# A new table of order, engines and buffers for a two-layer attention kernel

## The chip, the cores and the metric

The kernel runs on one core of one Trainium2 chip, in one launch. The metric is device time in microseconds (us), from the start of the program to its end. All inputs come from HBM and the result is written back to HBM.

## The reference, cut to what matters

Two kinds of layer alternate, A, B, A, B, each added to the residual `x` of 2048 tokens by 512 channels, all in bf16. Both have 32 heads of 16 channels.

```python
x = A_x
x = x + A(layernorm(x), wq, wk, wv, wo, beta)
x = x + B(layernorm(x), wqkv, w_phi, wo)
x = x + A(layernorm(x), ...)      # the same weights again
x = x + B(layernorm(x), ...)

def A(x, ...):                    # four segments of 512 tokens
    for s in range(4):
        p = softmax(q_s @ k_s.T / 4 + causal mask)
        a_dot = p @ v_s
        a_mem = phi(q_s) @ M / (phi(q_s) @ z + 1e-6)   # phi(t) = t+1 if t>0 else exp(t)
        out_s = g * a_mem + (1 - g) * a_dot            # g = sigmoid(beta), per head
        M, z = M + phi(k_s).T @ v_s, z + sum(phi(k_s))
    return concat(out) @ wo

def B(x, ...):                    # not causal: needs all tokens' keys first
    phi_q = [softmax(q @ w_phi), softmax(-q @ w_phi)]  # over 16 channels
    phi_k = the same of k
    kv, z = phi_k.T @ v, sum(phi_k)
    return (phi_q @ kv / (phi_q @ z + 1e-6)) @ wo
```

## The kernel before, in words

Tokens are cut into 16 tiles of 128, and four tiles make a segment. The residual X stays in SBUF for the whole program. `build` records every step as an operation of a graph (`Graph.op`), about 2,750 of them, with the tiles that it reads and writes. A helper records each kind, so that one source line stands for many operations: `mm` (L341) and `pair` (L356) record matmuls on TensorE (PE), `act` (L366) an activation on ScalarE (ACT), `evac` a copy from PSUM to SBUF that may stand on ACT (L374) or on VectorE (DVE, L375), `tr` (L383) a transpose by DMA issued from SyncE (SP), `dma` (L387) a store.

The work runs in this order. For each segment of layer A: layer norm (`ln`, DVE statistics L590 and L591, the root on GpSimd, POOL, L598 and L600, the scaling on DVE L607 or L611), a transpose of the normed tile, the projections to k, q and v (`a_proj`), then attention (`a_att`): scores by PE into a PSUM tile, the exponential on ACT from PSUM to SBUF (tiles p, pF and pE), the product with the values on PE, the division on DVE (L405, L878), the addition of the memory part (`oadd`, L882, on DVE or POOL), a transpose of the result by DMA, the output projection on PE and the addition to X (`res`, L926, on DVE). The keys of layer B (`b_keys`) follow in the same segment: PE, an exponential (`kexp`) on ACT, sums and products on DVE (L985, L405, L1007), and KV sums. Only after all four segments can the queries of layer B run (`b_query`): two exponentials of each pair of groups on ACT, the denominators (`zm`, `zs`, `zp`, L1060, L1061, L1065, with logarithms and exponentials on ACT between them), the numerator on PE, a multiplication on DVE (`nmul`, L1087 or L1090), the sum of its two halves (`nadd`, L1093, on DVE or POOL), a transpose by DMA, the output projection and the addition to X. In the last layer each finished pair of tiles is stored to HBM from SP's queue.

What sets the order is a table, `ORDER` (L1177): compressed numbers that hold, for all operations at once, their order, the engine of each, and the buffer that each tile gets in its pool. `Graph.place` unpacks it and `Graph.emit` writes each engine's instructions in that order; an instruction waits on semaphores for the operations that it depends on, and for those that last used its buffer. Each engine, SP's queue included, works its list strictly in order, so an instruction that waits holds up all behind it. PSUM is four buffers of 128 x 1024 f32 (pool pD, named D in the profile), through which every matmul's result goes. `keep` (L678) records six pairs of matmuls on constants whose result is not used.

Of the kernel before, what the change touches and what calls it, by code (L numbers as in the profile page):

```python
# [1181 lines left out]
N~t4_$F6bi<z53o~J690wr~2?ia0jg7GhT3ikjpgZ=!6_5pMV;y`>D<KHC!xjjIrq~CwK{I?GKfp)u1x&%Im>s@`V4Mt}!wj5>{V)UzV-f6&q4*7a1{+`sJcjkq8=K=d
_$_9|7MKkIXW?vYjrkFg(ZXgZfL*975w^h|)CyZ-Ps)xtup8yXT-YB6;8xfMyP!LT!H4(}#)E>m8>YfE_!y@{F&u(<aTDah@9=xfjfHR(48<8x9K&!Fj>ddg6iZ-9EQR
xMKCXsgI2;8^TmxU=TG$8sVI7plC$Ix{!XO-s({MUIg>k4b4W*@L@El&i1pJW};CNh!V{k0q!B=#j9#9$l5k}xhEQ{r^JkG(nI1xwCNLq@Ma1ZQ-s+gIwPz9`ri!m!@q
ea+>I#V<Z#A;X_zr-IP9*v^W6rWzg99n{taW1`vyZ9r%f>|`1fYVV8tcjJdGKS-K@CujVa!g1WDHA22*Eo#s;ZHc6(o+V?OZn(NKEQ{Vp9;_r8cH3gBR$0`SPOSxZpuS
DaThM2g|r7B;|eT7EAbKj1aF`q<)R!^n6lFgdP#*SCl#e))Q48#YFvYB@n_hCeW^0_qbjrx*W(7<h_R?Y6{qS{g9g!N+=9JmFm1)s)SF^c9EwY?X&aWLGE|BNQd!yv<!
AuSqxlpIw_{bRMo+xN$HrO|2W!$e+Cb%LJk_R+v>W&0KHQIWs3KLO3N(hsQeCP?Q|McWi|^nwoIn%l2Ra1r;xRmd&+!G;rxFx_lPD4!(9ei8nWoYKNKA`pF%dnapXg_L
Ls7VdmeMquPQ=WDC6DGY%p^!tC@rJqG=om!4%$hN=rM&+1cg&HZlSI81HQonn1~8-VLpiKXeF(tHFOBq(+WC_M{zA}qa(PTBsHYtcpCe1Ken`+8qq0iOq*ykoxxocNoV
mqp2H$sl>74l-a~uoC0@i;bOFcn1l~vc=?SG|L%q2Vr{Xl6nsae(zKX@TIA23Y*D(j@<euD%73bl+JeFIL=F(h(OR=JHJeUh`K_0^Sc_0sB%Z7uvB<JHYyq$M&T0TGrs
VoOk6KYLuXebZk={$qeaR#2uQ#d_0rDhZxMsZvi&O3P*kL1NXla}xyn#hy5Iklj+)Q%3*5jsgrc^Qx3dR(8QC>9)sV4BL)_!4gBEqs(N;}twb(KM55ac!Q%b+|5{fRiw  # L1190
bxAHc2Jew<VWd;i75K6=gc@Zb(xjc`T^9l~(B%G9!b7s!MEvY@7rwW{nv+`*=LshsUXXmP1j?41}>drm5AvfX%oRKe5EUv-T_%iL~ecYI9a&>-(E>RP1%4cae@8M?LoZ
~<;j?Me|0EhBgUdM4bE{AbANANkC&ntNqALb+!k5}^=PD;t>5Jz$p$LAEZfDdv?Dj?paV|1JfiWZ!Ts)!R*RYdbf{*hmCOTI!^sTFtRPTZNha1n8Yl_)B-Xw7Z7Ew|$h
Y=jk+L}jsw*Yi=XA!>?u_&Nz8#k+irU-M6Vg9?el;x2XN_MDo2<~N+2Qt*59KHa2Sbd8?zF-XYA`8nUA<4{Z_;18*|IKkCKCPq<RkZ>YMfG8nK3Kl2%6kp&{qO|ycI&e
1*7G*?;2o+)C8kZFZp`NHOF7hQl&1d*JzvPOdg7}nP@DCg=KB7-3Lfqh6TuamzpV1doN7NOcQ$rCgVu^C%D|!dc@;N@w<;A-YTf`9wMI!MrH4?Y!OKKrniUy*wXd;@5%
Y22CimMzcqC_&0PkcxDML*GBd{6hNjc6;rro<wN_=b9k-XgxZ$?-&TkwPR8-%?7EO2ieNL~4;nq!sBz2hmw{6z}m7I10@~bJ0q)7Pt8hzt3GnSMdRV$e(aK(O!JSpYmP
)j6dguFiZ>==|vxrL1YwP@W-4<^c6itW|2i?72U-EkwfGZ-9!&DNDLH%#W(yV=MuTa5b-U4%|k^V@jcg(BSbclU3|wQ#V9daj1gl+U0F}w5#z*oF+qIA_xL{F6%)lQF-
g>ydBtooSxga2#8fd&Oc!&+T=AZGUp(e{V!l`^W{72Cjd;Q<#7wbVtQG6UI&nih;00o#SR@vUo8lqg61T-lu}VDU)#4Fv6dS}QaYSquTf|neO>7rO#V%0*c8UgShj>T4
D|U-LVy`$Q8miOcm^d!Zhz4?>I3W&-lj5vsr1pygqOm$88p_M!oVX$mi>u<ixF9Zx>!OitEH8>%^0vGt?#K_sN8&^AvG_!MDn1i;Wi$D?_(HrVo607#xojc76km&$vXy
KtzY*Vxuf%uazIY%Wis#~e`MtO&+Q_!Doop{(h?nA#cr0Ft*Wv@206vtx<rC3I_LqI-Phx<4Dn62*$dBcx@-sP5elDMhpG6(@MtmVz{vf)@A4QNHBs)kUrBt%6s;5Ar>
?*s-`l_kY(#VdolO)+p1<MfGL`BJH`K1h%VKRYCD4VMms-?2h$$oOMj3r~sIPxnwL=KhVGD3bW6UoFfu8b#>$fPn-ek<e4Z)7r=T((lr<qP>zwpMM_kMfm#AXCV!a<+U  # L1200
ZQ_55_wM-*B%kDD0OeZtQoHCotE`N||Wezz<&Xx0IE}2_?Cws{6<vp24wpEYhV>v}8&<VBHM&Fk`WiL5azLxW))j!F0s+@E>kxs13%Q(7%tSA@AQZlX{Cflpwa)i99uB
p<ptSlo>t1jw^JfjxM%JQr_r=H5Ga+;hj&#Mb+oE$H^Dyfy8A!o{G@@F|n#nbWiNLf&hlB4AWIZ?im#pHE$Lk(7WC8!`BtcR#cvbZcMOUMptmOLZ#$wIQD>ZER}TdIIO
D=W!!vbXA^`l|DCjJ&9BtGnuwN}?~T_tX`YR7dDY9j3$eWO+w*R_kScnNerb@2d~g2DwRgQyJw(c|sahQkT;GREQ4MndC`%TAq@HWo*4jZk8!@N}W|_(~IR2IaDo`R;`
rDG%8Z8lI!I%Oogjxol3{jpQ+DPcAY~XmY=9k)hc;J9+mINVJeMYAy>=7x`@s!hpQ1Pt^Q7ZuTtxe)EXJ3)9H`ZH>#*iufJ8@RS#8E7t=jeY_&{gk@wVn)n66Yy;K}EK
@CtP^cU)}%B-{Kuhm-lNDWkR)eQZWdY~Svcxs~hQaw>KbzYrMSCLia$NCffR8^DJWp15E$5-p*CAm!sHAm0Ymt{_!OK+E3WCAry&(@RFRykQks7Mv1qSY0-L++G&<@@>
rT}V51RgP3as-PaFg4Jj>PLJ37WC2}7){y!21yA-D<%jB-N~k92nzELhsGqAz`h}XTcgbTimYS#El?$~}^R-rGbvZp<Pto(#0zFl~R3WOgE~BUE^16aPuP^Az`Uka0FV
_3zr}{Jfx&A`WR}0j1wObyLKdLIaq8_8J>l?a~4ppyIRsBYRMoqeus-{2GAL-JnjQU!Cqc7_#I*}@?j>{S9s?MNq>RY<De64;`*YqK|M<!NDRdsz)U(z#GIrUhVS0nWk
okXQp#*EU|R8R-yHCa)yKCQ3I8#28bt<UHcI+dEGW~-+<naZFts!S@25_+Y6rqAlJYMiQ}e^%#oW;I2PS2yKUbyvTqr>QUXSGuOIr5ox-y0)&Y8f#&sxub9Em-+|&y<V
# [65 lines left out]
```

## Time and profile before

| | before |
|---|---|
| time, three runs | 462.59 us median, 462.41 to 462.62 |
| span of the profiled execution, first to last instruction | 461.2 us |
| PE busy | 437.7 us, 95% |
| ACT busy | 420.3 us, 91% |
| DVE busy | 416.2 us, 90% |
| POOL busy | 80.1 us, 17% |
| granted TensorE clock | 0.998 on average |

Times in the profile count from the start of the span. A row of the timeline gives start, length, engine, source line, operation, written and read tiles (buffer numbers left out), and in square brackets how long the engine stood idle before it and what ended that. A row of the table by stretch gives the busy time of each engine inside the stretch; "(x...)" is a count of instructions. SPq is SP's queue, where only the issue of a DMA takes time; PEld is the loading of weights.

### The profile page before, as it was taken

What the parts mean: (1) busy time and instruction counts of PE and PEld (TensorE: products, weight loads), DVE (VectorE), ACT (ScalarE), POOL (GpSimd) and SP (SyncE); (2) the same over time, 40 slices, a digit from 0 to 9 for tenths busy, and PEclk for the clock granted to TensorE, in tenths of its full rate; (3) what the DMA queues carried; (4) which work ended last, traced back from release to release, by engine and by line L of the source; (5) the groups of instructions that cost most, each with busy time, mean ns of one, the idle gap of its engine ahead of it and who ended that gap; (6) DMA issues with size and microseconds to landing.
All of it is one profiled execution on the core that took longest, in us unless ns stands there. A gap on an engine that the chain in (4) does not pass through costs nothing.

```text
span 461.2 us, 25354 instructions
## 1 busy us (share of the span) xinstructions
PE 437.7 (95%) x11716; PEld 295.6 (64%) x11716; DVE 416.2 (90%) x807; ACT 420.3 (91%) x542; POOL 80.1 (17%) x160
## 2 busy tenths in 40 slices
PE   8989899899999999998899999999999999998896
PEld 4456667667776776675456677677677677666553
DVE  6989998898889999898999899998899889998896
ACT  4999999899999998789699999999999999878991
POOL 2402021101221211102532031130221023110020
PEclk9999999999999999999999999999999999999999
DMA  8554642552233322100243443264113321200357
GB/s 247 127 150 80 127 63 37 75 96 54 50 46 54 46 40 36 37 3 4 48 54 78 71 85 72 49 96 61 26 39 49 50 39 27 48 14 1 50 121 180
DMA packets 90058, 30.37 MB, mean 66 GB/s; under 512 B 76640, under 2 KB 89952, under 8 KB 89952
## 3 DMA queue, kind: packets, MB, share of 16 engines
q1 hardware_dynamic: 89520, 28.48, 33.3%
q8 instruction: 92, 1.51, 1.4%
q10 hardware_dynamic: 432, 0.27, 0.2%
q14 instruction: 14, 0.11, 0.1%
HBM read 6.32 MB, written 2.10 MB: 18 GB/s over the span
## 4 chain that ended last, share of the span: by engine, by line
PE 48%; ACT 40%; DVE 6%; DMA 3%; issue 2%; SPq 0%
PE D L356 31%; ACT p L366 21%; PE D L341 15%; ACT pF L366 13%; ACT pE L366 5%; DMA p<-p 2%; PE D L662 2%; DVE X L926 1%; DMA X<-in_A_x_dram 1%; DVE p L1090 1%; DVE p L375 1%; DVE stats L590 1%; ACT pS L366 1%; DVE p L611 0%; DVE pK L375 0%
## 5 line engine op out<-in xcount | busy, mean ns | idle before, releaser
L366 ACT ACTIVATE p<-D 128x1024 bf16<-128x1024 f32 (+2 forms) x224 | 216.0, 1004 | 13.5 <-PE D L356 9.7
L366 ACT ACTIVATE pF<-D 128x896 bf16<-128x896 f32 x128 | 116.7, 940 | 2.8 <-PE D L341 2.5
L341 PE MATMUL D<-pK,pQ 64*128 64x256 bf16 (+3 forms) x1536 | 112.9, 243 | 4.1 <-ACT pF L366 1.0
L341 PEld LDWEIGHTS D<-pK,pQ 64*128 64x128 bf16 x1536 | 55.2, 94 | 40.7 <-ACT pF L366 5.4
L341 PE MATMUL D<-pV,pF 64*128 64x34 bf16 x1024 | 73.8, 175 | 0.4 <-ACT p L366 0.4
L341 PE MATMUL D<-pW,pF 64*128 64x34 bf16 x1024 | 71.3, 175 | 0.0
L341 PEld LDWEIGHTS D<-pV,pF 64*128 64x128 bf16 x1024 | 55.3, 93 | 2.3 <-ACT p L366 0.7
L341 PE MATMUL D<-pV,p 64*128 64x34 bf16 x1024 | 53.3, 176 | 0.3 <-issue 0.2
L366 ACT ACTIVATE pE<-D 128x768 bf16<-128x768 f32 x64 | 52.3, 831 | 1.4 <-PE D L341 1.0
L341 PEld LDWEIGHTS D<-pW,pF 64*128 64x128 bf16 x1024 | 51.9, 93 | 0.9
L341 PE MATMUL D<-pW,p 64*128 64x34 bf16 x1024 | 52.1, 176 | 0.0
L598 POOL TENSOR_SCALAR rstd<-mv 128x1 f32<-128x1 f32 x60 | 16.1, 272 | 205.9 <-DVE mv L591 205.5
L341 PEld LDWEIGHTS D<-pV,p 64*128 64x128 bf16 x1024 | 47.0, 93 | 3.3 <-issue 0.9
L341 PE MATMUL D<-tri,two 64*128 64x128 bf16 (+1 forms) x384 | 46.7, 234 | 0.4 <-issue 0.4
L341 PEld LDWEIGHTS D<-pW,p 64*128 64x128 bf16 x1024 | 45.2, 93 | 1.3
L590 DVE BATCH_NORM_STATS2 stats<-X 128x6 f32<-128x512 bf16 x64 | 42.9, 680 | 3.0 <-DMA X<-in_A_x_dram 2.5
L341 PE MATMUL D<-pV,pE 64*128 64x34 bf16 x512 | 44.9, 175 | 0.4 <-issue 0.4
L926 DVE TENSOR_TENSOR X<-X,D 128x1024 bf16<-128x1024 bf16 (+1 forms) x36 | 39.4, 1095 | 5.7 <-PE D L356 5.0
L341 PE MATMUL D<-pW,pE 64*128 64x34 bf16 x512 | 42.5, 175 | 0.1
L985 DVE TENSOR_REDUCE pS<-p 128x64 f32<-128x1024 bf16 (+1 forms) x36 | 38.8, 1088 | 1.8 <-ACT p L366 1.8
L375 DVE CAST p<-D 128x512 bf16<-128x512 f32 x48 | 31.1, 683 | 6.3 <-PE D L356 6.1
L356 PE MATMUL D<-WB_o,p 64*128 64x512 bf16 (+1 forms) x288 | 33.0, 353 | 2.7 <-issue 1.3
(115 smaller groups left out, 988.9 us busy)
## 6 DMA issues: line engine op xcount, KB each, us to landing
pW<-pV SPq DMA_DIRECT2D x16, 136.0 KB, 3.1
out_dram<-X SPq DMA_DIRECT2D x7, 256.0 KB, 2.8
X<-in_A_x_dram SPq DMA_DIRECT2D x3, 512.0 KB, 6.1
pX<-in_B_wqkv_dram SPq DMA_DIRECT2D x3, 512.0 KB, 4.6
p<-p SPq DMA_TRANSPOSE x76, 2.8
pX<-p SPq DMA_TRANSPOSE x54, 3.2
WA_k<-in_A_wk_dram SPq DMA_DIRECT2D x2, 256.0 KB, 6.3
WA_q<-in_A_wq_dram SPq DMA_DIRECT2D x2, 256.0 KB, 7.0
```

The source lines that it names most:

```text
L341: ins = e.matmul(out_ap, lhsT, rhs, start=st, stop=sp, tile_position=(basep(lhsT), basep(out_ap)))
L356: ins = e.matmul(out_ap, lhsT[64 * hf:64 * hf + 64], rhs[64 * hf:64 * hf + 64], start=k == 0 and i == 0, stop=k == 1 and i == len(lists[hf ...
L366: return self.g.op({"act": (dur, lambda e: e.activation(out_ap(), in_ap(), func, scale=scale))}, reads, writes, opens, label=label)
L375: "dve": ((340 if fast else n / 0.96 + 65), lambda e: e.tensor_copy(out_ap(), in_ap()))}
L590: v(lambda e: e.bn_stats(self.stats[:, t, :], self.X[:, t, :]), 602, [R("X", t)], [R("st", t)], label="bn")
L598: v(lambda e: e.tensor_scalar(rs, self.mv[:, t, 1:2], LN_EPS, None, op0=ALU.add), 170, [R("mv", t)], [R("rstd", t)], eng="pool", label="rstd")
L662: ins = e.matmul(D.t[c0:, r0 * 8:r0 * 8 + n], r[:, c0:], ones(r, n), start=True, stop=True, tile_position=(r0, c0))
L926: self.v(lambda e: e.tensor_tensor(X(), X(), src(), ALU.add), 65 + 512 * n / 0.96, pr + xr, xr, label="res")
L985: fn = lambda e, sgn=sgn, eo=eo, Z=Z, n=n: e.tensor_reduce(Z.t[:, 0:64 * n].rearrange("p (k s h) -> p k s h", k=n, s=2)[:, :, sgn, :], eo( ...
L1090: v(lambda e, N=N, Tm=Tm, w=w, shape=shape: e.tensor_tensor(shape(Tm.t[:]), shape(N.t[:]), w(), ALU.mult), 1131, [N, AB[(0, 0)], AB[(0, 1) ...
```

## The change

The operations, their arithmetic and the shape of every tile stay as they are. The string `ORDER` is replaced: another order, other engines for some operations, other buffers. One line out and one line in:

```diff
 ORDER = """
-c-rlG1GFYtlWpMm8fDwIZQHhO+qP}n=q}rAn`L%ab=S-MZdXt9|9jTVd+W_wli$7hWu9{~V#kghk(u{qfQFD5k^n<eNCu6dF*JchkQ&lJIzUJPDIpbPg!E7oN<u9FC<w
+c-qx?1-Ko>mhO`B;}UmwcXxMpcXxMpcXxL;NFeSC5r{wn2~Gm>0GaN6lKTP|?(k;j&ih{NbGoZ)S1<Y3zgAc66u^)X0D?e3dPoTwAQd!()Q|?!L0V`8jiCu7h9r;_2%17cs0oFj88iok
...
 """
```

The stages follow each other as before; within them operations stand some places earlier or later. Of the operations that may stand on either of two engines these move: four evacuations from ACT to DVE (near 95, 174, 249 and 405 us of the old profile) and one from DVE to ACT (near 390 us), so ACT has 49 instead of 52; four `oadd` from DVE to POOL and two back, six `nadd` from DVE to POOL (four of them near 235 to 253 us, two near 433 to 437 us); three settings of constants from POOL to DVE in the first 20 us.

ACT in layer A of the first pass, near 86 to 97 us of the old profile (p, pF and pE from D are exponentials of scores or keys, p from pK the one of `phi`, pK from D by L374 an evacuated q). Before:

```order
L366 ACTIVATE pE<-D 128x4x192
L366 ACTIVATE p<-D 128x1024 x2
L366 ACTIVATE p<-pK 128x1024
L366 ACTIVATE pF<-D 128x2x448 x2
L366 ACTIVATE p<-D 128x1024
L366 ACTIVATE pE<-D 128x4x192 x2
L374 ACTIVATE pK<-D 128x512
L366 ACTIVATE pF<-D 128x2x448 x2
L366 ACTIVATE p<-D 128x1024 x2
```

The same place in the new order:

```order
L366 ACTIVATE pE<-D 128x4x192
L366 ACTIVATE p<-D 128x1024
L366 ACTIVATE pF<-D 128x2x448
L366 ACTIVATE p<-D 128x1024
L366 ACTIVATE p<-pK 128x1024
L366 ACTIVATE pF<-D 128x2x448
L366 ACTIVATE p<-D 128x1024
L366 ACTIVATE pE<-D 128x4x192 x2
L366 ACTIVATE p<-D 128x1024
L366 ACTIVATE pF<-D 128x2x448
L366 ACTIVATE p<-D 128x1024
```

The first of the two pF moved ahead of an exponential of keys and of the one of `phi`, and the evacuation of q (L374) left ACT. On PE, the scores of both pF now stand ahead of the last half of a projection of k (WA_k); before, the second stood behind it.

DVE in the last stage, near 432 to 436 us (L1087 is `nmul`, L1093 `nadd`, L375 an evacuation, L1060, L1061 and L1065 the steps of the denominators). Before:

```order
L1093 TENSOR_TENSOR p<-p 128x512
L1087 TENSOR_TENSOR p<-p,pS 128x1024
L1065 TENSOR_TENSOR pS<-p,pS 128x8x16 x2
L1093 TENSOR_TENSOR p<-p 128x512
L1087 TENSOR_TENSOR p<-p,pS 128x1024
L375 CAST p<-D 128x512
L1093 TENSOR_TENSOR p<-p 128x512
L1060 TENSOR_TENSOR p<-p,D 128x256
```

The new order there:

```order
L1093 TENSOR_TENSOR p<-p 128x512
L1087 TENSOR_TENSOR p<-p,pS 128x1024 x2
L1065 TENSOR_TENSOR pS<-p,pS 128x8x16 x2
L375 CAST p<-D 128x512
L1060 TENSOR_TENSOR p<-p,D 128x256
L1087 TENSOR_TENSOR p<-p,pS 128x1024
L1093 TENSOR_TENSOR p<-p 128x512
```

One `nadd` between the two `nmul` is gone (it stands on POOL now, whose list ends with four of them instead of two), and a step of the next denominator moved ahead of a `nmul`.

SP's queue at the end of the program (transposes of attention results, and stores of X). Before:

```order
L383 DMA_TRANSPOSE p<-p 128x4x128 x6
L387 DMA out_dram<-X 128x2x512
L383 DMA_TRANSPOSE p<-p 128x4x128
L387 DMA out_dram<-X 128x2x512
L383 DMA_TRANSPOSE p<-p 128x4x128 x6
L387 DMA out_dram<-X 128x2x512
L383 DMA_TRANSPOSE p<-p 128x4x128
L387 DMA out_dram<-X 128x2x512 x3
L387 DMA out_dram<-X 128x512
L387 DMA out_dram<-X 128x2x512
L387 DMA out_dram<-X 128x512
```

The new order there:

```order
L383 DMA_TRANSPOSE p<-p 128x4x128 x11
L387 DMA out_dram<-X 128x2x512 x2
L383 DMA_TRANSPOSE p<-p 128x4x128 x3
L387 DMA out_dram<-X 128x2x512 x4
L387 DMA out_dram<-X 128x512
L387 DMA out_dram<-X 128x2x512
L387 DMA out_dram<-X 128x512
```

The first two stores now stand behind eleven transposes, and no store stands ahead of the last transpose any more except those two. Four of the six `keep` stand among the last matmuls, one of them between the two halves of the very last output projection.

More of the change, by code (lines that the diff above doesn't have):

```diff
@@ L1182 @@
[L1182 to L1189, printed above, removed]
@@ L1234 @@
[L1234 to L1235 removed]
+c-qx?1-Ko>mhO`B;}UmwcXxMpcXxMpcXxL;NFeSC5r{wn2~Gm>0GaN6lKTP|?(k;j&ih{NbGoZ)S1<Y3zgAc66u^)X0D?e3dPoTwAQd!()Q|?!L0V`8jiCu7h9r;_2%17cs0oFj88iok
+l290mKrN^ZEubZ|g4R$9N<&2`3U#0^NGJo9pfXf}HqaK@L3`)`WuYT<g3izdia|Xn4ke%*lm`t}p&HbO>QDhrKwdZr4WKJ@gBs8s3?zaZFbu-s6L4?^K7vzl8qPs}I1kAn7hHfd&;#;;
@@ L1236 @@
+$Z-D@X)rvHKpyfDXfYV0Fd)|BKFM$hgoz@(H1dcQIAn$dNaS-Oz$XZc3TX6mEKsA-2ph~Hq<kK5%(NGIPdWLIdAd<XggVbJLXQj>2s%@!$G4z>Q-102QaMmEf;lo=c$z{2R15PIb6|rK
+a8(AI00@D@aKI`r`Gr?J3@V=sew}929&w_<#ZZtaBnVk^s5jwL)LRk+QLI2hz#WjDp0EhNc6s55@);88R}61WfQcR&f%Nd|lJ6b{wxr&)L<82#Y7f0IPX_zwc&fcHIu7LkJ3Q8@AfKOJ
+1OmFfB=Ry)P_&O7ym>2V6h;JcHAr$``|3SGUXfuLiXqxhY3ILa!k8kIA4Xv#1Z$6M;XXAe459=@cq_?E2xUA92+5&>RU`y^w2AVn18M6QVTICog(TFg!sIa$Opw1z3ey}VJyiWQ3IggQ
+4Ey$Z;{OB3h?q$
 """
```

98 lines of the change are left out of this document (48 added, 50 removed).

## The prediction

> **What bounds the kernel now.** I read the page first, then the busy time by stretches, then the waits and the timeline at the places where an engine stands still. From the page, the span, the busy time and the chain that ended last:
>
> ```profile
> span 461.2 us, 25354 instructions
> PE 437.7 (95%) x11716; PEld 295.6 (64%) x11716; DVE 416.2 (90%) x807; ACT 420.3 (91%) x542; POOL 80.1 (17%) x160
> PE 48%; ACT 40%; DVE 6%; DMA 3%; issue 2%; SPq 0%
> ```
>
> Three engines are nearly full at once, and the chain changes between PE and ACT. An average hides which of them decides where, so I cut the span at the borders of the stages. Each row has the stretch, its length, and the busy time of PE, weight loads, DVE, ACT and POOL:
>
> ```profile
> 0.00:30.00 30.00, 26.79 (x360) 14.12 (x360) 24.49 (x66) 21.86 (x35) 8.89 (x32) 1.00 0.72 197
> 30.00:180.00 150.00, 143.62 (x4374) 102.18 (x4368) 136.62 (x255) 147.19 (x179) 21.55 (x40) 1.00 0.37 62
> 180.00:235.00 55.00, 51.47 (x1186) 32.22 (x1182) 50.21 (x97) 43.67 (x69) 13.04 (x23) 1.00 0.11 23
> 235.00:400.00 165.00, 162.91 (x4712) 114.47 (x4710) 151.34 (x294) 162.77 (x199) 32.55 (x60) 1.00 0.34 57
> 400.00:450.00 50.00, 46.05 (x1034) 29.12 (x1025) 45.81 (x90) 43.86 (x63) 4.07 (x6) 1.00 0.26 50
> 450.00:461.20 11.20, 6.82 (x88) 3.54 (x88) 7.74 (x9) 0.99 (x2) 0.00 (x0) 0.93 0.71 179
> ```
>
> The two attention stretches (30 to 180 and 235 to 400 us) are bound by ACT: its idle time there is 150 - 147.19 = 2.81 us and 165 - 162.77 = 2.23 us. No order can win more there than these 5.0 us and what work leaves ACT. Between them, in the queries of layer B, ACT is idle 11.33 us, PE 3.53 and DVE 4.79: a mixed stretch, bound by hand-overs. After 450 us the engines run dry.
>
> **ACT loses work.** The only price in work that the change has on ACT is that of the moved evacuations. Rows of the groups and of the timeline, three such evacuations in a row on ACT, and the same copy on DVE:
>
> ```profile
> L374 ACT ACTIVATE pK<-D 128x512 bf16<-128x512 f32 x10 | 5.7, 608 | 0.0
> 14.48 1.55 ACT L374 ACTIVATE pK<-D 128x512 bf16<-128x512 f32 x3
> L375 DVE CAST p<-D 128x512 bf16<-128x512 f32 x48 | 31.1, 683 | 6.3 <-PE D L356 6.1
> ```
>
> One lasts 0.61 us by itself, but three in a row take 1.55, so one costs ACT 1.55 / 3 = 0.52 us. Two leave ACT in the first attention stretch (near 95 and 174 us): 2 x 0.52 = **-1.0 us**, on the path, because ACT binds that stretch. On DVE they cost 2 x 0.68 = 1.4 us, hidden in its 150 - 136.62 = 13.4 idle us of the stretch; without that cover they cost up to 1.4 - 1.0 = 0.4 us net. In the second attention stretch one leaves (249 us) and one comes (390 us): 0. The fourth (405 us) leaves where ACT has 6.1 idle us of 50: 0. Bounds of this term: -1.6 (if the third counts too) and +0.4.
>
> **The longest wait of ACT in attention.** It is at 92 us, 1.46 of the 2.81 idle us. The timeline, rows of PE and ACT:
>
> ```profile
> 89.11 1.05 ACT L366 ACTIVATE p<-pK 128x1024 bf16<-128x1024 bf16 x1
> 89.61 0.61 PE L356 MATMUL D<-pX,WA_k 64*128 64x512 bf16 x4
> 90.05 0.91 ACT L366 ACTIVATE pF<-D 128x896 bf16<-128x896 f32 x1
> 91.53 0.61 PE L356 MATMUL D<-pX,WA_k 64*128 64x512 bf16 x4 [1.31 <-issue]
> 91.96 0.37 PE L341 MATMUL D<-pK,pQ 64*128 64x256 bf16 x4
> 92.42 0.92 ACT L366 ACTIVATE pF<-D 128x896 bf16<-128x896 f32 x1 [1.46 <-PE D L341]
> ```
>
> PE stops for 1.31 us in the middle of eight equal matmuls, and the profile shows no wait for it ("issue"). The scores that ACT needs next stand behind them. The table doesn't remove this stop, since it isn't a wait in the program. But the new order puts both scores ahead of that half projection, so with the stop at the same place ACT would have an exponential of keys, the one of `phi` and the second pF (0.9 to 1.05 us each) to do while PE stands. That would win all 1.46 us. If the stop falls elsewhere, it may meet an ACT without stock, and nothing is won. I take the middle, **-0.7 us**, with ends 0 and -1.5.
>
> **The head.** DVE stands still for a load, and an evacuation that PE and then ACT need stands behind it. The timeline:
>
> ```profile
> 21.16 0.58 SPq L474 DMA_DIRECT2D X<-in_A_x_dram  x1
> 26.23 0.69 DVE L590 BATCH_NORM_STATS2 stats<-X 128x6 f32<-128x512 bf16 x1 [1.53 <-DMA X<-in_A_x_dram]
> 28.66 0.81 ACT L366 ACTIVATE pE<-D 128x768 bf16<-128x768 f32 x1 [0.73 <-PE D L341]
> ```
>
> SP issues the third block of X behind four transposes. In the new table this load stands ahead of them, so DVE's 1.53 us of waiting should go. But the new order also puts other DVE work, two more statistics and a mask product among it, ahead of the same evacuation. So of ACT's 0.73 us I take **-0.3 us** (ends 0 and -0.7). The tri mask copy that PE waits for near 17 us moves to the start of DVE's list; ACT has work there, so I count it at nothing.
>
> **The last stage.** DVE and ACT are both almost full there, and two `nadd` leave DVE. The stretch, and the same addition on both engines:
>
> ```profile
> 430.00:445.00 15.00, 13.90 (x358) 8.02 (x356) 14.50 (x30) 14.60 (x21) 2.43 (x2) 1.00 0.54 105
> L1093 DVE TENSOR_TENSOR p<-p 128x512 bf16<-128x512 bf16 x16 | 6.8, 422 | 0.1
> L1093 POOL TENSOR_TENSOR p<-p 128x512 bf16<-128x512 bf16 x10 | 12.3, 1231 | 65.1 <-DVE p L1090 33.2 <-DVE p L1087 31.6 <-DVE nb L605 0.2
> ```
>
> DVE saves 2 x 0.42 = 0.84 us. ACT, with 0.4 us idle in 15, is late next, so only half of it shows: **-0.4 us** (ends 0 and -0.8). The two results come 1.23 - 0.42 = 0.81 us later to their transposes; PE, idle 1.1 us there, hides that. Four more `nadd` leave DVE near 235 to 253 us, but there ACT binds again, so I count them at nothing; without that they are worth up to 4 x 0.42 = 1.7 us, less 0.68 for the evacuation that DVE takes over.
>
> **The end.** The last transpose, the last projection and the last additions to X:
>
> ```profile
> 451.17 0.42 DVE L1093 TENSOR_TENSOR p<-p 128x512 bf16<-128x512 bf16 x1
> 452.10 0.58 SPq L387 DMA_DIRECT2D out_dram<-X  x1
> 453.12 1.19 SPq L383 DMA_TRANSPOSE p<-p  x1
> 453.12 3.71 DMA p<-p
> 456.39 1.22 DVE L926 TENSOR_TENSOR X<-X,D 128x1024 bf16<-128x1024 bf16 x1 [0.17 <-PE D L356]
> 456.88 1.29 PE L356 MATMUL D<-WB_o,p 64*128 64x256 bf16 x16 [0.53 <-DMA p<-p]
> 458.21 0.69 DVE L926 TENSOR_TENSOR X<-X,D 128x512 bf16<-128x512 bf16 x1 [0.59 <-PE D L356]
> p<-p SPq DMA_TRANSPOSE x76, 2.8
> ```
>
> The source is ready at 451.59, the transpose is issued only at 453.12 behind a store, and lands 3.71 us later, where the median is 2.8. With the store behind it, it can be issued at 452.1 and land near 454.9 instead of 456.83. What is late next is DVE, whose addition to X ends at 456.39 + 1.22 = 457.61 and is followed at once by the last one, which now starts at 458.21: 0.6 us won. The `keep` between the two halves of the last projection has that slack. **-0.6 us** (ends 0 and -1.0).
>
> Sum against the profiled execution: -1.0 - 0.7 - 0.3 - 0.4 - 0.6 = -3.0 us, a span of 458.2. The median of the runs stands 462.59 - 461.2 = 1.4 us above the span, so **459.6 us**. The terms' ends together give -5.6 and +0.4, that is 457.0 to 463.0.
>
> **A lock against the added POOL work.** In the old trace an addition on POOL and a product on DVE that both work in SBUF lengthen each other:
>
> ```profile
> 383.74 0.68 DVE L1007 TENSOR_TENSOR pT<-p,pT 128x1024 bf16<-128x1024 bf16 x1
> 383.91 1.53 POOL L882 TENSOR_TENSOR p<-p 128x512 bf16<-128x512 bf16 x1 [8.02 <-DVE p L795]
> 384.92 1.07 DVE L1007 TENSOR_TENSOR pT<-p,pT 128x1024 bf16<-128x1024 bf16 x1
> ```
>
> The product took 1.07 us instead of 0.68. [...]
>
> **The rivals.**
>
> *New waits on ACT (chance 0.16, slower).* The attention stretches have only 5.0 idle us of ACT, 1.5% of 315. The new order exchanges neighbours on PE and ACT all along them; if the scores come late for ACT often enough to double this idle time, the cost is +5.0, with the 0.7 of the middle term not won: 462.6 - 1.0 - 0.3 - 0.4 - 0.6 + 5.0 = 465.3 us. It decides the sign from 2.3 us of added idle time. For it speaks that nothing stands ready there: each wait costs at once. Against it: in the old order ACT's waits there have few causes, the largest of them no fault of the order.
>
> *The lock (0.06, slower).* Six of the additions moved to POOL stand where DVE is full (four near 235 to 253 us, two near 435). If each holds DVE up for a whole addition, 1.23 us by the row of L1093, DVE loses 6 x 1.23 = 7.4 and saves 6 x 0.42 = 2.5: +4.9, and the -0.4 is gone: 459.6 + 0.4 + 4.9 = 464.9 us. At the row's 0.39 each the loss of 2.3 and the saving cancel, and the forecast stands but for its 0.4.
>
> *Queries improve too (0.16, faster).* In 180 to 235 us PE is idle 3.53 us. One kind of these waits, from the list of who waited for whom (total, times, longest), is for DVE's step of the denominators:
>
> ```profile
> PE D L341 <- DVE p L1060: 1.4, 2, 1.0
> ```
>
> If the order closes all 3.53 us as well, 459.6 - 3.5 = 456.1 us. Against it: the new rows there differ from the old by exchanged neighbours only, and the chain from the denominators to the numerator keeps its length.
>
> *Nothing (0.10).* The waits that go come back one place further, behind PE or DVE: 462.6 us.
>
> **How the numbers follow.** The forecast has 0.52. About 0.2% (0.9 us) is what a measurement of this kernel can tell from no change. Forecast and improved queries are faster: 0.68. Nothing: 0.10. Waits and lock are slower: 0.22. The range starts a little below the improved queries, 455.8, and reaches to the lock, 464.9, which leaves out most of the waits' case and little else.
>
> **What would show it.** ACT's idle time in the first attention stretch should be near 2 us; the stop of PE should leave ACT busy; the third block of X should land before DVE asks for it; the last transpose should follow its source at once, and the last two additions to X should stand back to back. The forecast is wrong if ACT's idle time in the attention stretches grows, if additions on POOL stand beside DVE instructions that take twice their usual time, or if the queries' stretch takes more than 55 us.

## The result, and the profile after

The changed kernel takes 475.02 us (median of 4 runs, 473.67 to 475.57) beside 462.50 us (461.00 to 462.62) of the kernel before on the same chip: the ratio is 1.026, 95% interval 1.021 to 1.032. It is slower by 12.5 us where 3 us less were forecast, and lies far outside the range. From the page of after, the span, the busy times and the chain that ended last:

```profile
span 473.2 us, 25355 instructions
PE 444.0 (94%) x11716; PEld 297.9 (63%) x11716; DVE 420.8 (89%) x805; ACT 420.2 (89%) x539; POOL 90.7 (19%) x165
PE 64%; ACT 23%; DVE 8%; issue 2%; DMA 2%; SPq 0%; DVEq 0%
```

ACT has the same work as before (420.2 instead of 420.3 us), DVE 4.6 us and PE 6.3 us more busy time, though no operation was added (in the two stretches at the half clock, 232.06 to 235.47 and 443.68 to 447.09 us, PE is busy for 3.33 and 3.41 us, and eight matmuls of 64x512 take 1.78 to 1.90 us in them and 1.03 elsewhere; so about half of PE's 6.3 us come from the clock, by estimate); and the chain has passed from ACT (40% before) to PE. The stretches, in the same columns as before (the two attention stretches, the queries of layer B between them, and the last stage):

```profile
30.00:180.00 150.00, 141.34 (x4269) 99.73 (x4263) 135.62 (x253) 144.07 (x174) 25.15 (x45) 1.00 0.39 61
180.00:235.00 55.00, 50.89 (x1204) 32.57 (x1202) 49.69 (x92) 42.52 (x64) 13.13 (x22) 0.97 0.12 22
235.00:400.00 165.00, 159.17 (x4431) 108.70 (x4428) 147.17 (x282) 157.47 (x192) 35.39 (x61) 1.00 0.35 55
400.00:450.00 50.00, 47.19 (x1120) 32.61 (x1118) 45.37 (x83) 43.12 (x59) 6.91 (x11) 0.97 0.19 29
```

ACT's idle time in the attention stretches is now 5.93 and 7.53 us, 13.5 instead of 5.0. These rows cover the same times, and after does less of the work in them; with their borders moved by the lag shown below (30 to 183.3 and 240.8 to 411 us), the same work has 7.0 and 5.9 us of ACT's idle time, 7.9 us more than before. Two entries of PE's clock column have fallen to 0.97.

Since both kernels do the same 2748 operations, each operation's start can be compared one by one. The table gives the lag: how much later the operations of PE, ACT and DVE start in after than in before, as the median over those that before starts in each slice of 10 us (us, one execution of each):

```
slice of before  30   60   90  130  140  180  210  220  230  250  260  280  320  370  400  430  450
lag of after   -0.3  0.2 -1.0 -0.8  1.7  3.3  3.3  4.3  5.8  6.9  8.1  8.7  9.9 10.4 11.0 11.7 11.0
```

The loss comes in steps: 2.5 us near 140, 1.6 by 180, 2.5 in the queries, 2.9 by 280, then steps of about a microsecond. Three things stand at these steps, where PE, ACT or DVE waits.

**PE stops with nothing to wait for.** The largest step, rows of PE and of ACT in after:

```profile
139.09 0.17 PE L341 MATMUL D<-pV,pF 64*128 64x34 bf16 x1
141.12 0.39 PE L341 MATMUL D<-pK,pQ 64*128 64x256 bf16 x4 [1.86 <-DVE p L649]
```
```profile
141.55 1.02 ACT L366 ACTIVATE p<-D 128x1024 bf16<-128x1024 f32 x1 [1.53 <-PE D L341]
143.17 0.92 ACT L366 ACTIVATE pF<-D 128x896 bf16<-128x896 f32 x1 [0.60 <-PE D L341]
```

The wait is put down to DVE, but the DVE work on which this score depends (`Macc` 549 last) had ended at 138.44, and the trace has nothing else that it depends on. What ended then is in the list of DMA queues, whose columns are packets, MB and share; it reads the same in both kernels:

```profile
q8 instruction: 92, 1.51, 1.4%
```

92 packets of 16384 B for 11716 matmuls and as many weight loads, 23432 / 92 = 255 of them to a packet. I take the queue for that of PE's own program, one piece per 128 matmuls with their loads; this is read from the places of the stops. Counted in matmuls, the stops without a reason stand at the border of such a piece, and PE goes on 2.2 to 3.4 us after the packet's start. Counted in all of PE's instructions (matmuls, weight loads, waits for semaphores), 102 of the 103 stops over 0.25 us in the eighteen traces of this case stand where the count modulo 256 is 193 to 196. Six of them:

```
kernel  last matmul (no.)   packet starts   PE goes on   packet to PE
before   89.84 (2129)           88.23          91.53         3.30
before  144.16 (3660)          142.21         144.74         2.53
after    49.31 (985)            47.99          50.51         2.52
after   139.09 (3531)          138.70         141.12         2.42
after   256.80 (6202)          255.28         257.74         2.46
after   328.32 (8240)          326.82         329.33         2.51
```

The "issue" stop at 92 us, on which a term of the prediction rests, is one of these. Before has four, 3.1 us; after has eight, 6.8 us (from the start of the last matmul to the start of the next, less 0.15 us for each stop; the idle time that the profile gives is 2.8 and 6.2 us). These are two executions: of the other kernels that keep the whole old order, the profiles have none to four such stops (none in e8, three in e13 and g1, four in g4 and e9, two in e11), and of those with the whole new order three to eight (e10 and e12 three, e5 four, e2 six, e1 eight). The names are those of the experiments below.

**POOL additions stop DVE.** Rows of DVE and of POOL in after:

```profile
261.26 1.23 DVE L649 TENSOR_SCALAR p<-pK 128x1024 bf16<-128x1024 bf16 x1
262.42 1.38 DVE L649 TENSOR_SCALAR p<-p 128x1024 bf16<-128x1024 bf16 x1
```
```profile
259.95 3.56 POOL L1093 TENSOR_TENSOR p<-p 128x512 bf16<-128x512 bf16 x3
```

Both DVE rows take 0.42 us elsewhere. The second ends 0.29 us after POOL's last addition (263.51). Eight DVE instructions of after are longer so, by 6.1 us in all, five of them by 0.88 to 0.97 us (the expectations below say nine, by a miscount). Such a meeting is called a lock here. In before an addition does this once by 0.39 us and once by 0.15 (L611 at 390.78); three more lengthened instructions, near 17 and 18 us, stand beside POOL's fillings of constants.

**Transfers arrive later.** `otr` 866, the transpose ahead of the projection `Wo` 867, was issued at 135.09 and landed 2.45 us later in before. In after its sum comes from POOL at 134.86, and SP is busy with others, since for the transpose at 126.76 it had waited while the four behind were ready:

```profile
126.76 1.20 SPq L383 DMA_TRANSPOSE pX<-p  x1
128.00 2.13 SPq L741 DMA_DIRECT2D pW<-pV  x1
130.17 1.30 SPq L383 DMA_TRANSPOSE p<-p  x1
131.53 0.60 SPq L741 DMA_DIRECT2D pW<-pV  x1
132.25 6.63 SPq L383 DMA_TRANSPOSE p<-p  x4
```

It is the last of the four, issued at 137.55 and landed at 141.76, 4.21 us later. `Wo` starts at 141.85.

### The profile page after: what moved, and what is told of

It is laid out like the page before. It is cut to its first block, busy times and chain, and to the rows that moved or that the text cites. A ratio compares the mean times of both kernels' runs of the same rounds, so it can differ in the third digit from the quotient of the medians.

```text
span 473.2 us, 25355 instructions
## 1 busy us (share of the span) xinstructions
PE 444.0 (94%) x11716; PEld 297.9 (63%) x11716; DVE 420.8 (89%) x805; ACT 420.2 (89%) x539; POOL 90.7 (19%) x165
## 4 chain that ended last, share of the span: by engine, by line
PE 64%; ACT 23%; DVE 8%; issue 2%; DMA 2%; SPq 0%; DVEq 0%
PE D L356 41%; PE D L341 23%; ACT p L366 12%; ACT pF L366 7%; ACT pE L366 2%; DMA X<-in_A_x_dram 1%; DVE p L1090 1%; DVE p L1087 1%; DMA p<-p 1%; DVE X L926 1%; DVE p L649 1%; DVE pT L1007 1%; DVE stats L590 1%; ACT pS L366 1%; ACT pX L374 0%
## 5 line engine op out<-in xcount | busy, mean ns | idle before, releaser
L598 POOL TENSOR_SCALAR rstd<-mv 128x1 f32<-128x1 f32 x60 | 17.4, 292 | 256.1 <-DVE mv L591 252.5
L590 DVE BATCH_NORM_STATS2 stats<-X 128x6 f32<-128x512 bf16 x64 | 42.9, 680 | 3.0 <-DMA X<-in_A_x_dram 2.6
L985 DVE TENSOR_REDUCE pS<-p 128x64 f32<-128x1024 bf16 (+1 forms) x36 | 38.7, 1086 | 2.3 <-ACT p L366 2.2
L600 POOL TENSOR_TENSOR rstd<-rstd,mhalf 128x1 f32<-128x1 f32 x60 | 36.4, 612 | 3.5
L375 DVE CAST p<-D 128x512 bf16<-128x512 f32 x49 | 32.0, 681 | 5.2 <-PE D L356 4.8
```

Of the source, the lines that this page charges most:

```text
L375: "dve": ((340 if fast else n / 0.96 + 65), lambda e: e.tensor_copy(out_ap(), in_ap()))}
L590: v(lambda e: e.bn_stats(self.stats[:, t, :], self.X[:, t, :]), 602, [R("X", t)], [R("st", t)], label="bn")
L598: v(lambda e: e.tensor_scalar(rs, self.mv[:, t, 1:2], LN_EPS, None, op0=ALU.add), 170, [R("mv", t)], [R("rstd", t)], eng="pool", label="rstd")
L600: v(lambda e: e.tensor_tensor(rs, rs, self.mhalf[:], ALU.pow), 540, [R("rstd", t), R("mhalf")], [R("rstd", t)], eng="pool", label="rstd")
L985: fn = lambda e, sgn=sgn, eo=eo, Z=Z, n=n: e.tensor_reduce(Z.t[:, 0:64 * n].rearrange("p (k s h) -> p k s h", k=n, s=2)[:, :, sgn, :], eo( ...
```

## The experiments

Names of operations are the code's labels with the number of the operation. `e`- and `g`-kernels are built from the two tables; where one takes an order from one table and buffers from the other, a tile whose buffer isn't free gets the one that was free longest.

**Is a piece of program the limit?** Two kernels on the old table. In the first, PE runs 1024 tiny matmuls at its end:

```diff
+            for _ in range(m):              # m = 512 in one keep, else 0
+                for hf in range(2):
+                    r = self.onesb[64 * hf:64 * hf + 64, :]
+                    ins = e.matmul(D.t[:, 512 * hf:512 * hf + 34], r, r[:, 0:34], start=True, stop=True, tile_position=(64 * hf, 0))
```

> The kernel before, with one `keep` moved to the end of PE's order and 1024 tiny matmuls (64 rows, 34 columns, two row groups at a time) put into it, so that PE runs eight pieces of its program with nothing else to do. Theory H (a piece of program takes a fixed time): 128 matmuls take 3.3 to 3.5 us instead of 128 x 12.6 ns = 1.6, with one stop of about 1.7 us per 128 matmuls, some 27 us in all and a span near 488 us. Rival: PE runs them at 12.6 ns as it runs those of `PV`, 13 us, a span near 474 us.

Its time is 487.3 us (one run), its span 484.8. PE at the end of the timeline, and its queue:

```profile
462.01 1.77 PE L682 MATMUL D<-onesb 64*128 64x34 bf16 x128 [1.81 <-issue]
465.48 2.00 PE L682 MATMUL D<-onesb 64*128 64x34 bf16 x128 [1.71 <-issue]
468.95 2.00 PE L682 MATMUL D<-onesb 64*128 64x34 bf16 x128 [1.48 <-issue]
472.42 2.00 PE L682 MATMUL D<-onesb 64*128 64x34 bf16 x128 [1.48 <-issue]
```
```profile
q8 instruction: 99, 1.62, 1.4%
```

128 matmuls, a stop, 128 matmuls: one piece per 3.47 us here, and 3.74 to 4.02 in the three that follow. The first row's work is at full clock (1.77 us), the others' at one half (2.00, from 464.3 us on), and the stop fills up the rest. So theory H of this run holds for short pieces in a row: PE stopped at each piece's end, 3.47 to 4.02 us per 128 matmuls. A single short piece was faster: in before, at 426.4 us, the packet started 0.24 us behind the border, and the piece took 2.59 us with its stop.

The second moves only the borders of the pieces, by 64 matmuls:

```diff
-                for rows, n, m in ((64, 51, 12), (64, 64, 8), (64, 256, 4), (128, 34, 8)):
+                for rows, n, m in ((64, 51, 44), (64, 64, 8), (64, 256, 4), (128, 34, 8)):
```

> The kernel before, with 64 tiny matmuls (64 rows, 51 columns) more among those that warm the clock at the start, nothing else. By the trace, PE's program comes in pieces of 16384 B, one per 128 matmuls, and PE goes on 2.3 to 2.7 us after the packet's start. Theory H: with the borders 64 matmuls earlier the stops at 49.5, 89.8, 144.1 and 428.3 us go (3.3 us), and new ones come wherever 128 matmuls between the new borders took less than 3.35 us, by the old trace near 60, 125, 163, 170, 209, 305, 318, 331 and 396 us, together 10.7 us: 464 to 470 us. Rival N: the stops belong to their places in the order; they stay, and the 64 matmuls cost at most 64 x 12.6 ns = 0.8 us: 462.5 to 463.4 us.

477.57 us (476.51 to 480.71), ratio 1.032 (1.028 to 1.036): 15 us slower for 64 tiny matmuls in the first microseconds, more than theory H of this run gave. Its list of waits, and that of before (total, times, longest):

```profile
PE D L341 <- issue: 11.5, 17, 1.6
```
```profile
PE D L341 <- issue: 1.6, 6, 0.5
```

19 stops, 14.1 us, and none at 49.5, 89.8, 144 or 428. Of the nine places that the expectation named, eight have a stop (209 has none), and eleven stops stand where none was named. These rows answer to 60 and 125:

```profile
61.22 0.20 PE L341 MATMUL D<-pV,p 64*128 64x34 bf16 x2 [1.47 <-issue]
...
125.45 0.19 PE L341 MATMUL D<-pW,p 64*128 64x34 bf16 x2 [1.00 <-issue]
```

These stops are 11 us longer than those of before, whose span is 13.6 us shorter. The old table's time thus rests on where the borders fall, and no edge of the program says so.

**Do the locks and the clock cost?** In after, seven additions that stop DVE are done on DVE (602, 1040, 1393, 1645, 1656, 2231, 2588), everything else stays. The change had moved four of them to POOL (the expectation counts three); 1040, 1393 and 1645 stood on POOL in before too:

> The kernel after, with the seven additions that stop a DVE instruction in its trace (two `oadd` and one `nadd` of those that the change moved, among them) done on DVE, at the same places of the order. Theory H: the 6.1 us by which nine DVE instructions were longer go, 7 x 0.42 = 2.9 us of additions come, DVE has 3.2 us less to do, and the time falls by 1.5 to 3.2 us: 471.8 to 473.5 us, with no DVE instruction of twice its usual time. Rival N: DVE is not what the stages wait for, 474.5 to 476 us.

474.44 us (472.52 to 476.02), 0.6 less than after, within the spread of both. The instructions are short again, as this row of its DVE shows beside the one above:

```profile
262.22 0.42 DVE L649 TENSOR_SCALAR p<-p 128x1024 bf16<-128x1024 bf16 x1
```

Its lag grows by 0.8 us from 230 to 270 where that of after grows by 2.4; but it grows by 3.0 instead of 0.9 at 170 to 180, where `Wo` 1066 waits 2.29 us for its transpose (1.30 in after). What was won at one place was lost at another, and theory H of this run is not borne out in the total.

The loss at 180 comes from the edit itself. An addition put on DVE at its old place in the order comes after all that DVE has ahead of it: `oadd` 1040, which POOL had ended at 165.67 us in after, ends at 175.13 on DVE. SP issues the transposes in order, so the transpose of its sum holds the next one, for `Wo` 1066, whose sum was ready at 174.20. Rows of DVE and of SP in e2, then of SP in after:

```profile
174.72 0.41 DVE L882 TENSOR_TENSOR p<-p 128x512 bf16<-128x512 bf16 x1
```
```profile
175.16 3.05 SPq L383 DMA_TRANSPOSE p<-p  x2
```
```profile
171.56 4.58 SPq L383 DMA_TRANSPOSE p<-p  x2
```

So e2 takes the locks away and adds a delay, and what the locks alone cost in time stays open.

The clock, by moving four `keep` in after, and by taking them out of the last stage in before:

```diff
 PE of after:   Wo2 1407, N 1526, +keep 2742, xnTp 1297, +keep 2744, xnTp 1305 ... N 2566, +keep 2746, N 2585, +keep 2743, N 2676 ... -keep (four, at the end)
 PE of before:  -keep 2742, 2746, 2744, 2743 in the last stage ... Wo 2729, +keep 2746, Wo2 2730, +keep 2744, 2742, 2743
```

> The kernel after, with four of its six `keep` matmuls at other places of PE's order: two between the transposes of layer B's last `xn` (near 229 and 230 us), two ahead of `N` in the last stage (near 440 and 441 us); in the new table these four stood at the very end. Theory H (hidden costs: the 12 us come from costs that no edge of the program shows, namely PE's clock at one half in two stretches of 3.4 us, POOL additions that stop DVE, and PE's own program arriving late): both half-clock stretches go, 2 x 1.7 = 3.4 us less, 471.6 us. Rival N (new neighbours: the new order itself hands the operands over later, and the half clock falls where PE waits anyway): 474.3 to 475.0 us, the clock at 1.0 or not.

> The kernel before, with four of its six `keep` matmuls at the end of PE's order, where the new table has them. Theory C (the clock costs time): without them PE's clock falls to one half for 3.4 us between 425 and 450 us, as in after, and 1.0 to 1.7 us are lost, 463.5 to 464.3 us. Rival: the clock falls too, but in a stretch in which DVE and ACT set the pace, and less than 0.4 us is lost: 462.3 to 462.9 us.

e1: 475.94 us (473.91 to 477.18), no gain. The half clock in the last stage is gone (it comes at 468.9 now), the one in the queries stays, at 233.4. e8: 462.23 us beside 461.72 of before in the same comparison, ratio 1.002 (1.000 to 1.003), though the clock falls at 426.9 for 3.4 us, as forecast:

```profile
420.00:430.00 10.00, 7.58 (x306) 5.47 (x303) 7.52 (x18) 9.85 (x18) 0.00 (x0) 0.84 0.07 15
```

ACT is busy for 9.85 of these 10 us: the slow clock fell where PE is little waited for. The loss is 0.7 us by the ratio (0 to 1.5), nearer to the rival than to theory C; so in the old order moving the four `keep` costs at most 0.3%. What it costs in the new order, e1 doesn't tell apart from nothing.

**Do transfers in a bunch cost?** In after, SP's queue at one place; and in before, two transposes that are needed late moved out of a bunch:

```diff
 SP of after:   foldT 187, +vsw 813, +PhKtr 505, +vsw 812, +PhKtr 504, xnT 709, -(these four, among) otr 842, otr 923, otr 866
 SP of before:  xnT 761, -foldT 189, otr 579, otr 603, -foldT 187, vsw 542, xnT 767, xnT 773, PhKtr 505, vsw 541, +foldT 189, +foldT 187
```

> The kernel after, with two places of SP's queue changed: `vsw` 813 and 812 and `PhKtr` 505 and 504, whose sources are long ready, ahead of the transpose `xnT` 709 for which SP waits until 126.73 us, and `otr` 1041 ahead of `xnT` 972 for which it waits until 169.02 us. Theory T (transfers in a bunch): a transfer that waits holds the ready ones behind it, they then go together, and whatever shares the DMA engines with them comes late: the transpose `otr` 866 (4.21 us instead of 2.45) and the packet with PE's program (3.1 us after the border instead of 0.9). The 2.03 us stop of PE at 139 us falls under 0.7, the waits of `Wo` 867 and of `Wo` 1066 (0.50 and 1.36 us) go, 471.8 to 473.2 us. Rival S (short pieces): the 128 matmuls ahead of that stop took 3.5 us and the next piece is late in any case; the stop stays over 1.5 us, 474.3 to 475.3 us.

> The kernel before, with the transposes `foldT` 189 and 187, which are needed only at 150 and 171 us, behind `vsw` 541 in SP's queue instead of at 86.15 and 90.95 us. Theory T: the packet with PE's program, which started 2.16 us after the border at 86.07 us, then starts about 1 us after it, the stop of 1.68 us at 89.84 us falls under 0.6, and the time falls by about 1.1 us, to 461.4 us: faster than both kernels. Rival S: the piece is late because PE is through with 128 matmuls too soon; the stop stays, 462.6 us.

e5: 476.08 us (471.92 to 476.63), ratio 1.030: no gain in the median. The execution that was profiled is the lowest, 471.92. In it `Wo` 867 waits no more, and the stop stays, shorter:

```profile
140.18 0.39 PE L341 MATMUL D<-pK,pQ 64*128 64x256 bf16 x4 [1.17 <-DVE p L649]
```

The packet started 2.3 us after the border instead of 3.1. So part of theory T is seen there and part of S, and the other four runs, 2 to 4.7 us longer, have no profile. This stays open. The expectations of e5 and e10 name a second place, `otr` 1041 ahead of `xnT` 972; the kernels don't have it. SP's rows of e5 show the transposes of `xn` still ahead, and `Wo` 1066 still waits 1.19 us, so that half of theory T is untested:

```profile
167.65 2.51 SPq L383 DMA_TRANSPOSE pX<-p  x2
170.20 4.58 SPq L383 DMA_TRANSPOSE p<-p  x2
```

e9: 461.94 us, ratio 1.000 (0.998 to 1.002). The stop at 89.8 is 0.86 us instead of 1.68, as theory T has it, but the time doesn't fall. The reason came from kernels whose table is that of before up to this place: their stop there took 0.53 (e8), 0.53 (e13 below), 0.58 (g1) and 0.86 us (g3). The 1.68 us of before's profile were the ill luck of that one execution, and e9's 0.86 us prove nothing for theory T.

The repairs of e2 and of e5 together:

> The kernel after with two edits together: SP's queue changed at two places (`vsw` 813 and 812 and `PhKtr` 505 and 504 ahead of `xnT` 709, `otr` 1041 ahead of `xnT` 972), and the seven additions that stop a DVE instruction done on DVE. Theory D (the loss is a sum of separate costs): transfers 1.9 us and locks up to 3.2 us come off, 470 to 472 us. Rival M (a kernel this full moves its waits): where one stop of PE goes, its program's next piece comes due elsewhere, and the sum of these stops stays near 5 to 7 us: 473.5 to 476 us.

473.69 us (470.81 to 476.92), 1.3 us below after, with the intervals of the ratios overlapping (1.020 to 1.027). Three stops of PE (3.2 us) instead of eight, locks 0.2 us instead of 6.1, and yet 11 us slower than before in the median (8.3 us in the execution with the profile): rival M in time. It is no clean test of a sum, since it has the delay of `oadd` 1040 too (ended at 174.38; `Wo` 1066 waits 1.91 us) and SP's second place not at all.

**Which part of the change costs?** The engines of the new table on the old order, and the old engines on the new order:

> The kernel before, its order and buffers kept, with the engines of the new table: ten additions go to POOL, two come back, three evacuations leave ACT and one comes. Theory P (the prediction's own terms): two evacuations leave ACT in the first attention stretch, -1.0, and DVE gets rid of 8 x 0.42 us net, -0.4 in the last stage: 460.4 to 461.2 us. Theory L (the lock): an addition on POOL that starts ahead of a DVE instruction on SBUF alone stops it for the rest of its 1.15 us, as nine times in after; with three to six such meetings 463 to 467 us.

> The kernel after, its order and buffers kept, with the engines of the old table. Theory L: the locks of the moved additions go (3.0 us of DVE), 472 to 473.5 us. Rival O (the order itself, by the places at which PE's program runs dry and SP's queue bunches): 474 to 477 us, with six to nine such stops of PE again.

e11: 470.11 us (468.05 to 472.37), ratio 1.017 (1.014 to 1.020). e12: 480.36 us, ratio 1.037 (1.035 to 1.040). Each half alone is worse than before, and the order with the old engines is worse than the whole change. Part of that comes as in e2, from an addition that changes its engine at the same place in the order: the largest step of e12, 6.0 us at 140, is `oadd` 865, which ends at 141.23 on DVE (134.86 on POOL in after), so that `Wo` 867 waits 3.94 us. Exchanging engines alone is thus no neutral step. Nor were the buffers tried alone: 1081 of the 1498 tiles have another buffer in the new table, and e12 took them over with the order. In the traces PE's waits that end with a buffer's release come to 6.1 us in before and 7.1 in after, from 30 us on.

In e11 the largest step of the lag (2.7 us) is at 235 to 242 us, rows of DVE, POOL and PE:

```profile
237.09 1.11 DVE L605 SCALAR_TENSOR_TENSOR nb<-mv,rstd 128x1 f32<-128x1 f32 x1
```
```profile
234.80 3.38 POOL L1093 TENSOR_TENSOR p<-p 128x512 bf16<-128x512 bf16 x3 [0.23 <-DVE p L1090]
```
```profile
242.53 1.04 PE L356 MATMUL D<-WB_o,p 64*128 64x512 bf16 x8 [2.46 <-DMA p<-p]
```

Three additions in a row on POOL; `nb`, 0.15 us elsewhere, takes 0.96 longer under the lock, as theory L has it. PE's 2.46 us are not the lock's: the sum that they wait for was ready at 235.95, but its transpose (`otr` 1518) was issued at 238.33, behind that of a sum which, second on POOL, ended at 237.06 (235.71 on DVE in before). PE went on 4.20 us after that issue.

The engine moves one kind at a time:

```diff
 g1:  529 Qev2 act -> dve,  989 BVe act -> dve
 g4:  oadd 602, 865, 1975, 2231 and nadd 1521, 1649, 1656, 1663, 2588, 2670 dve -> pool;  oadd 1121, 2349 pool -> dve
```

> The kernel before, with only the two evacuations of the first attention stretch that the new table takes off ACT (`Qev2` 529 near 95 us, `BVe` 989 near 174 us) done on DVE. The prediction's first term: ACT binds there, 2 x 0.52 = 1.0 us less, 461.5 us beside 462.5 of before. Rival (PE sets the pace there, by its program's pieces and its hand-overs): within 0.4 us of before.

> The kernel before, with only the additions at the new table's engines (ten go to POOL, two come back to DVE), the evacuations as before. Theory L: an addition takes 1.15 instead of 0.42 us on POOL and stops DVE when it starts ahead of it, and its transpose and projection wait; most of the 7.6 us that all engine moves cost together, 467 to 470 us. Rival: the evacuations cost it, 462 to 464 us here.

g1: 462.69 us beside 462.50, ratio 1.001 (1.000 to 1.003): the evacuations win nothing. g4: 465.32 us, ratio 1.008 (1.006 to 1.010): the additions cost 2.8 us, less than theory L gave. The other moves of e11 (three evacuations and three fillings of constants; in all four evacuations leave ACT and one comes, where the expectation says three) were not tried alone; with the 0.2 of g1 and the 2.8 of g4 they leave 4.6 of its 7.6 us.

**Is the loss a sum over places?** Up to 204 us in after and 201 us in before both have done exactly the same operations, so the tables can be joined there; and after's start up to 130 us with before's rest:

> The table of after for everything that starts before 130 us in its trace, and the table of before for the rest (30 tiles get another buffer, since the two tables leave different ones free). Theory H: the 1.2 us that after is ahead between 90 and 130 us are kept and nothing of the later losses comes, 461.4 us, with the new places of PE's stops from 130 us on as in before. Rival N: the lead is a debt of the order, paid back behind the border in any case, 462.6 us or more.

> The table of after up to 204 us, that of before from there (the same operations are done at the seam; 54 tiles get another buffer). Sum over places: by the increments of one execution after is 3.2 us behind at that point, 465.7 us. Rival (the whole table): under 463.5 or over 468 us.

> The table of before up to 201 us, that of after from there (50 tiles get another buffer). Sum over places: the 12.5 us less the 3.2 of the first half, 471.2 to 471.8 us. Rival (the whole table): under 469 or over 474 us.

e4: 467.59 us, ratio 1.011 (1.007 to 1.015). g2: 470.45 us, 1.017 (1.015 to 1.020). g3: 476.32 us, 1.031 (1.028 to 1.033). Both halves together lose 21.8 us, not 12.5, so the medians are no plain sum. The lag of each shows where the rest is:

```
slice of before    30   90  130  140  180  200  210  230  260  280  320  400  450
after            -0.3 -1.0 -0.8  1.7  3.3  3.2  3.3  5.8  8.1  8.7  9.9 11.0 11.0
e4 (130)          0.2 -0.6 -0.3  3.9  4.1  4.1  4.1  4.1  4.2  4.2  4.5  4.4  4.4
g2 (204)          0.3 -0.6 -0.7  3.3  5.0  4.9  6.5  6.5  7.7  7.7  8.1  8.0  8.8
g3 (201)          0.8  0.2  0.3  0.2  0.1  2.6  4.6  8.6 10.5 10.8 11.5 12.5 12.7
```

Away from a seam each piece of table behaves as in its own kernel: the old table loses only 0.5 us more behind it in e4 (from 140) and 1.1 in g2 (from 240), the new one makes its step near 140 again in g2 (4.0 us), and loses 4.1 us from 230 on in g3 (5.2 in after). The seams themselves cost: 2.8 us in g2 (at 210 and 240), some 6 us in g3 beyond the 2.6 that after loses there, and in e4 `Wo` 867 waits 3.0 us behind transposes that the old table expects done earlier. So the steps seem bound to places in the table; their sizes in one execution are not to be added up to better than some microseconds.

**The end by itself**, in before:

```diff
 SP:  otr 2671, -store 2579, otr 2666, +store 2579, -store 2593, otr 2618, +store 2593 ... otr 2719, otr 2714, -store 2689, otr 2728, +store 2689
```

> The kernel before, with three stores behind the transposes that follow them in SP's queue (2689 behind the last `otr`, 2593 and 2579 behind one each); the prediction's term on the end by itself. Theory E: the last transpose is issued about 1 us sooner and PE's waits for `otr` in the last 15 us (2.9 us in the trace of before) shrink by 0.6 to 1.2 us: 460.5 to 461.3 us beside 461.7 to 462.5 of before. Rival: the transposes then meet each other on the DMA engines and land after 4.0 us instead of 2.45, nothing is won: 461.6 to 462.5 us.

462.54 us beside 462.51, ratio 0.999 (0.997 to 1.001): nothing. The last transpose is issued at 451.86 instead of 453.12, but this execution is 1.4 us ahead from 90 us on. Counted from its sum, the transpose is issued after 1.32 us instead of 1.52 and takes 4.07 us instead of 3.71; PE's waits for `otr` from 430 us on are 2.7 us in all, 2.3 in before. No kernel of this study is faster than before.

## Why the prediction was wrong

The step that failed is the sum itself: it prices five places, with ACT as the pace, and puts all the other exchanges of neighbours at nothing, since the old waits "have few causes". In their place PE's idle time grew by 5.7 us (from 23.5 to 29.2) and ACT's in attention by about 8 us, and no term that was priced came as a gain clear of the noise. What each cause costs in time stays open. Step by step:

*"ACT loses work", -1.0.* Wrong. g1 does just this and is no faster (ratio 1.001, 1.000 to 1.003). So work taken off ACT here buys no time, though ACT is idle for only 2.8 of 150 us. The likely reason is that PE, with 6.4 us idle, was held by hand-overs and by its own program, and that ACT's work fitted in beside it; in after the chain is PE's by 64%. That reason is argued and not shown.

*"The longest wait of ACT in attention", -0.7.* This step failed worst. I saw rightly that the stop is "no wait in the program", and then treated it as a fixed feature of the place that the new order may hide. The stops stand at the borders of the pieces (102 of 103), and 64 matmuls more at the start moved them in e3; whether transfers beside them move them too stayed open. So after does not stop at 92, and has eight other stops, 6.8 us, in its one profile. The stop nearest to that place, at 85.87, leaves ACT idle for 0.40 us. And its size was that of one execution: kernels with the same table there lost 0.5 to 0.9 us. The lead of about 1 us that after has from 90 to 130 us is no gain of the change: g1 and g4, with the old order, have 0.4 to 0.7 and 1.0 in the same slices.

*"The head", -0.3.* The lag is -0.3 us at 30, and the wait of 0.73 us at 28.66 is gone from ACT's rows, as is DVE's of 1.53 us for the load; a new one of ACT, 0.61 us, stands at 25.40. The size is that of the noise, since kernels with the same start lag by -0.3 to 0.3 us there, so this is no proof.

*"The last stage", -0.4.* Wrong in sign. One of the two `nadd`, 2588, stops `zp` in after; in g4 the same addition takes 0.69 us from `nmul`, and the lag of g4 grows by 0.6 us from 420 to the end, in one execution.

*"The end", -0.6.* Wrong. e13 moves the stores as I described and nothing is won; the issue came 0.2 us sooner after its sum, and the transpose, with others under way, took 0.36 us longer. In after the last transpose is issued 1.09 us behind its sum and takes 4.22 us, and the last two `Wo` wait 0.57 and 0.89 us for theirs.

*The lock, "0.39 each", rival at 0.06.* Mis-sized: five times in after the lock cost DVE 0.88 to 0.97 us, nearly a whole addition of 1.15. I had one row, of a late start, and took its price for all. The rival's 1.23 us for each of six additions, from which the range's upper end comes, was a supposition that no trace of before shows; in after eight DVE instructions were longer, by 0.2 to 0.97 us. The rival's price was near (DVE lost 6.1 us against 7.4), its places in part (three of the eight, at 261, 262 and 444 us). What that costs in time is not settled: all the additions of g4 cost 2.8 us.

*"New waits on ACT", 0.16.* This rival names what came: ACT's idle time in the attention stretches grew by about 8 us, and it decides the sign from 2.3. Its argument against itself, that the old waits "have few causes", failed: the causes (piece borders, the lock, SP's queue) are there in both kernels, and the old table meets them less often.

The prediction's own sign of error, "if the queries' stretch takes more than 55 us", came too: there the lag grows by 2.5 us, with `nb` stopped for 0.91 us by an addition at 225.1, PE's transposes of `xn` waiting 2.5 us in all instead of 1.3, and the clock at one half from 232.06 to 235.47.

What stays open: how the 12.5 us divide. Repairs of locks and of SP's queue together gave 1.3 us, within the noise, and the repair of the locks brought a delay of its own; the stop at 139 came back in every kernel with the new table there but e4 and e12, where `Wo` 867 waited instead, 3.0 and 3.9 us; and the remaining engine moves, the buffers, and `otr` 1041 ahead of `xnT` 972 were not tried alone.

## What to carry to other kernels

Where three engines are full and the work is cut into hundreds of short hand-overs, a table of order is worth what its luck with the unmodelled costs is worth: any exchange of neighbours can move all of them, and an edit costed at nothing may still cost (64 tiny matmuls 15 us in e3): none of the edited kernels of this study came out faster. A stop in which an engine waits for nothing should be placed before it is priced: count instructions to it, look at the engine's own program queue, and look at the same stop in a second execution. And a term read from one execution, smaller than what that execution's stops vary by, belongs in the range, not in the sum. Last, an operation that is moved to another engine at the same place of the order ends when that engine gets there (`oadd` 1040 at 175.13 us on DVE, at 165.67 on POOL): work out its new end, and who waits for it, before you call the move a test of one cost.
